# Agent attention and a squared-ReLU feed-forward on one core: other fixed steps for the attention's matmuls among the feed-forward's

## Chip, cores and metric

One core of a Trainium2 chip runs the whole program. The metric is the device time of one execution in microseconds (us), as the median of several runs; lower is better.

## What is computed

Attention goes through 49 agent rows per batch (B = 4, N = 12480, C = 128), and its output feeds a two-layer network with 2048 hidden units:

```python
def _attn_ref(q, k, v, agents):
    scale = 1.0 / np.sqrt(q.shape[-1])
    def sm(a, b):
        s = scale * (a @ b.transpose(0, 2, 1))
        e = np.exp(s - s.max(-1, keepdims=True))
        return e / (e.sum(-1, keepdims=True) + 1e-09)
    agent_v = sm(agents, k) @ v
    return (sm(q, agents) @ agent_v)

h = x @ w_in                      # x: attention's output, 49920 x 128
r = np.maximum(h, 0.0)
out = (r * r) @ w_out
```

## The kernel before

The kernel never forms the attention's output. For each batch it multiplies `agent_v` by `w_in` once (`w_make`), which gives weights with 49 rows, and the feed-forward's first matmul then runs on the softmax of the queries' scores.

**The main loop** (lines 586 to 597) has NG = 832 steps. Step i runs `mm1(i)`, 6 matmuls of 480 columns in row halves, then `relu` on ScalarE (ACT), and at odd i `square` on ACT, `high` and `low` on VectorE (DVE), which split the squares in a rounded part and a rest. `mm2` follows LAG = 5 steps later with 12 matmuls. 16 steps (NF) are a *group*: 960 queries, two output tiles of 8 steps (NJ) each. I count *places* 0 to 15 in a group from the step in which `mm2` begins its first output tile: step = 5 + 16 g + place. `mm2` begins an output tile at places 0 and 8, and `store` takes it at 7 and 15: a copy on ACT, an addition on DVE (L398), a DMA from SP.

**The two PSUM pairs.** `pairs` (line 145) are two tiles of two banks. While `mm2` sums an output tile in one, the other is the scratch of every attention matmul (`bank`, `use`, line 388); at the next output tile they change roles. So an attention matmul on the scratch pair waits until the reader of the one before has finished; the first in an output tile waits for `store`'s addition; and `mm2` of the next output tile waits for the reader of the last.

**The attention's steps**, each a matmul on PE and its reader:

- `q_scores` (32 matmuls in the profile, L167), read on DVE by `q_shift`: a maximum (L299) and a subtraction (L304). Then `q_exp` (ACT), `q_inverse` (DVE, L315 to L320), `q_norm` (GpSimd, L323), `q_hi` (ACT), `q_lo` (GpSimd, L330).
- `q_transpose`, row turning (16 matmuls, L338), read on ACT by `q_copy` (two copies, L342); then two DMAs `q_spread` (L347) make the half-swapped copy `p_b`.
- `k_scores` (L167), read on ACT by `k_copy` (L174), then `k_pmax` on DVE.
- `v_acc`, the sum of values of one tile of 960 rows (16 matmuls, L226), read on DVE by `v_sum` (L240 the first of a batch, L242 the others). Ahead of it go `v_hi` (ACT), `v_lo` (DVE, L218), `k_sub`, `k_lo` (GpSimd), `k_exp`, `k_hi` (ACT).
- `w_make` (L277), read by four copies on ACT (L283) and four subtractions on DVE (L285); `k_max` and `a_final` are short.

**The order** is fixed in advance: functions are put at step numbers by `at`, sorted, and recorded in that order, and every engine runs its own instructions in it. `chain` (line 417) places a list of operations one after another: each goes at least `hop` steps behind the one before, ACT and DVE get at most one attention operation a step (`taken`), and a PE operation is only put in a step of the set `slots`. A PE operation's reader must come in the next step. An attention operation stands at step + 0.5, behind that step's `mm2`. `plan_tokens` (line 447) plans a group's queries, with `q_load` 6 steps ahead of the scores; `plan_batch` (line 457) plans the next batch's keys, values and weights, and the batch after it starts where the values end. Two of the lines:

```python
    slots = {i for i in range(LAG, NG) if (i - LAG) % NJ in (1, 3, 5)}
        plan_tokens(s, (s - 2) * NF + NF // 2 + LAG)
```

So before, the places 1, 3, 5, 9, 11, 13 are open to all kinds. In the order that comes of it `q_scores` stands at 9 and `q_transpose` at 1 in every group; of 39 `v_acc`, 12 stand at 3, 4 at 5, 18 at 11 and 5 at 13; `k_scores` stand at 3, 5 and 11, `w_make` at 11 and 3.

Of the kernel before, what the change touches and what calls it, by code (L numbers as in the profile page):

```python
# [25 lines left out]
def agent_attention_relu2_kernel(ctx: ExitStack, tc: tile.TileContext, qT, kT, v, agT, w_in, w_out, outT):  # L26
# [12 lines left out]
    NF = F // P  # L39
    NJ = NF // 2  # L40
# [310 lines left out]
    NG = NSG * NF  # L351
# [50 lines left out]
    LAG = 5  # L402
# [3 lines left out]
    def at(t, f, *args):  # L406
        steps.append((t, len(steps), f, args))
# [3 lines left out]
    hop = {"PE": {"PE": 1, "ACT": 1, "DVE": 1}, "ACT": {"PE": 2, "ACT": 1, "DVE": 0, "POOL": 0, "SP": 0},  # L411
           "DVE": {"PE": 2, "ACT": 1, "DVE": 1, "POOL": 1, "SP": 0}, "POOL": {"PE": 3, "ACT": 2, "DVE": 2, "POOL": 1}}
    ends = {i for i in range(NG + LAG) if i >= LAG and (i - LAG) % NJ == NJ - 1}
    slots = {i for i in range(LAG, NG) if (i - LAG) % NJ in (1, 3, 5)}
    taken = {(e, i) for i in ends for e in ("ACT", "DVE")}

    def chain(t, todo):

        first = prev = None
        while todo:
            n = 1
            while todo[0][0] == "PE" and n < len(todo) and todo[n][1] in reads_bank and todo[n][0] != "PE":
                n += 1
            t += hop[prev][todo[0][0]] if prev else 0
            while True:
                g, p, ts = t, None, []
                for e, *_ in todo[:n]:
                    g += hop[p][e] if p else 0  # L430
                    while (e, g) in taken or (e == "PE" and g not in slots):
                        g += 1
                    ts.append(g)
                    p = e
                if todo[0][0] != "PE" or ts[-1] <= ts[0] + 1:
                    break
                t += 1
            for (e, f, *args), g in zip(todo, ts):
                taken.add((e, g))
                at(g + .5, f, *args)  # L440
            first = ts[0] if first is None else first
            prev, t, todo = p, ts[-1], todo[n:]
        return first, t
# [3 lines left out]
    def plan_tokens(s, base):  # L447
        todo = [("PE", q_scores, s), ("DVE", q_shift, s), ("ACT", q_exp, s), ("DVE", q_inverse, s),
                ("POOL", q_norm, s), ("ACT", q_hi, s), ("POOL", q_lo, s),
                ("PE", q_transpose, s), ("ACT", q_copy, s)]  # L450
        first, end = chain(base, todo if s > 1 else todo[2:])
        if s > 1:
            at(first - 6, q_load, s)
        at(end + .9, q_spread, s)
        assert end + 3 < s * NF, (s, end)

    def plan_batch(b, base):

        end = b * NS * NF
        for n in range(NS):  # L460
            if b == 1 and n < AHEAD:
                continue
            first, t = chain(base + int(n * 4.6), [("PE", k_scores, b, n), ("ACT", k_copy, n), ("DVE", k_pmax, n)])
            at(max(base, first - 8), k_load, b, n)
            if n == NS - 2:
                chain(t + 1, [("DVE", k_max, 0)])
        _, t0 = chain(t + 1, [("DVE", k_max, 1), ("PE", k_max, 2), ("DVE", k_max, 3), ("PE", k_max, 4), ("DVE", k_max, 5)])
        free = {}
        d = (end - 37 - t0) / NS
        for n in range(NS):  # L470
            t, r = t0 + 1 + int(n * d), free.get(n - 2, 0) + 1
            first, _ = chain(max(t - 2, r), [("ACT", v_hi, n, 0), ("DVE", v_lo, n, 0)])
            _, t2 = chain(max(t - 1, r), [("ACT", v_hi, n, 1), ("DVE", v_lo, n, 1)])
            at(first - 6, v_load, b, n)
            _, t1 = chain(max(t, r - 3), [("POOL", k_sub, n), ("ACT", k_exp, n), ("ACT", k_hi, n), ("POOL", k_lo, n)])
            _, t = chain(max(t1 + 3, t2 + 2), [("PE", v_acc, n), ("DVE", v_sum, n)])
            free[n] = t - 1
        _, e = chain(t + 1, [("DVE", a_final, 0, b), ("PE", a_final, 1, b), ("DVE", a_final, 2, b)])
        for f in range(0, F // 512, 2):
            _, e = chain(e + 2, [("PE", w_make, b, (f, f + 1), 0), ("ACT", w_make, b, (f, f + 1), 1), ("DVE", w_make, b, (f, f + 1), 2)])  # L480
        assert e + 2 < end, (e, end)
        return t + 1
# [95 lines left out]
        at(t - 2 + .1 * x, wo_split, 3, x)  # L578
    plan_tokens(1, 0)
    for s in range(2, NSG):  # L580
        plan_tokens(s, (s - 2) * NF + NF // 2 + LAG)
    t = 0
    for b in range(1, B):
        t = plan_batch(b, t)
# [41 lines left out]
```

## Time and profile before

| | |
|---|---|
| runs | 1997.25, 1997.75, 2004.7 us (median 1997.75) |
| profiled execution | 1994.79 us, of it 1993.0 us from first to last instruction |
| mean granted TensorE clock | 0.996 of full |
| TensorE busy | 1963.5 us |
| VectorE busy | 1762.7 us |
| ScalarE busy | 1725.0 us |
| GpSimd busy | 308.2 us |
| DMA | 129.56 MB, 65 GB/s on average |

The main loop begins at about 74 us and fills the rest. Its stages: in groups 0 to 38 the next batches' work is done beside the queries', three times keys, then values, then weights; from group 39 (1545 us) on only queries' work is left. A busy TensorE is one that has a matmul in its pipeline; a wait for a semaphore shows as idle time only beyond the matmuls still in flight.

### The profile page before, as it was taken

The numbers are of one execution on the slowest core, as the hardware profiler recorded it, in microseconds if no ns is written. First come the engines' busy times: TensorE is split into PE (matmuls) and PEld (weight loads), VectorE is DVE, ScalarE is ACT, GpSimd is POOL, SyncE is SP. The second block draws the span as 40 slices with busy tenths as digits, with TensorE's granted clock in tenths as the row PEclk, the third lists the DMA queues.
The fourth block names the chain that finished last, engine by engine and source line by source line (L and its number), as shares of the span: only waits on it lengthen the run. The fifth ranks groups of instructions, "written<-read, shape, count | busy, mean of one in ns | idle before, by whom it ended". The sixth has DMA issues, their size and how long they took to land.

```text
span 1993.0 us, 45859 instructions
## 1 busy us (share of the span) xinstructions
PE 1963.5 (99%) x20130; PEld 1852.2 (93%) x20130; DVE 1762.7 (88%) x1513; ACT 1725.0 (87%) x1818; POOL 308.2 (15%) x199
## 2 busy tenths in 40 slices
PE   9999999999999999999999999999999999999999
PEld 8699989999889999999979999899998999999998
DVE  7788899999888889999987888999998989888887
ACT  2588899998888889999988889899998999999997
POOL 0100122331000003332100000232210101010110
PEclk9999999999999999999999999999999999999999
DMA  8422122121122122122122212222211111111110
GB/s 289 122 84 81 43 76 74 54 76 54 44 85 83 48 61 74 48 81 64 43 66 69 73 54 70 60 64 68 62 47 37 34 51 29 51 33 51 34 42 21
DMA packets 52849, 129.56 MB, mean 65 GB/s; under 512 B 5761, under 2 KB 21249, under 8 KB 52649
## 3 DMA queue, kind: packets, MB, share of 16 engines
q1 hardware_dynamic: 52648, 126.62, 22.1%
q8 instruction: 158, 2.59, 0.5%
q14 instruction: 43, 0.34, 0.1%
HBM read 81.47 MB, written 25.56 MB: 54 GB/s over the span
## 4 chain that ended last, share of the span: by engine, by line
PE 74%; DVE 10%; ACT 10%; issue 5%; DMA 0%; DVEq 0%; SPq 0%; ACTq 0%
PE pair L392 40%; PE h L364 22%; PE pair L167 7%; ACT rg L373 4%; ACT rg L370 4%; DVE gl L381 3%; DVE gh L377 3%; PE pair L338 2%; DVE vs L218 1%; PE pair L226 1%; PE h L167 1%; PE pair L277 1%; PE pair L494 1%; DMA vt<-v 0%; DVE e L304 0%
## 5 line engine op out<-in xcount | busy, mean ns | idle before, releaser
L370 ACT ACTIVATE rg<-h 128x960 f32<-128x960 f32 x832 | 806.3, 976 | 193.3 <-PE h L364 191.9
L381 DVE TENSOR_TENSOR gl<-rg,gh 128x1920 fp32r<-128x1920 f32 x416 | 916.1, 2202 | 19.0 <-DVE gh L377 0.5
L373 ACT ACTIVATE rg<-rg 128x1920 f32<-128x1920 f32 x416 | 758.0, 1822 | 6.1
L392 PE MATMUL pair<-gh,wo_hi 64*128 64x480 f32 x3328 | 681.6, 377 | 5.7 <-DVE acc L240 5.1
L392 PE MATMUL pair<-gh,wo_lo 64*128 64x480 f32 x3328 | 682.4, 378 | 0.0
L377 DVE CAST gh<-rg 128x1920 fp32r<-128x1920 f32 x416 | 518.2, 1246 | 149.8 <-ACT rg L373 144.2
L364 PE MATMUL h<-p_b,w_hi 49*128 49x480 f32 x1664 | 643.4, 387 | 0.0
L364 PE MATMUL h<-p_a,w_hi 49*128 49x480 f32 x1664 | 640.6, 387 | 0.2
L392 PE MATMUL pair<-gl,wo_hi 64*128 64x480 f32 x3328 | 522.5, 376 | 0.4 <-DVE gl L381 0.3
L392 PEld LDWEIGHTS pair<-gh,wo_hi 64*128 64x128 f32 x3328 | 362.5, 184 | 23.1 <-DVE acc L240 6.4
L392 PEld LDWEIGHTS pair<-gh,wo_lo 64*128 64x128 f32 x3328 | 365.4, 186 | 16.5
L392 PEld LDWEIGHTS pair<-gl,wo_hi 64*128 64x128 f32 x3328 | 355.2, 185 | 15.9 <-DVE gl L381 1.2
L364 PEld LDWEIGHTS h<-p_a,w_hi 49*128 49x128 f32 x1664 | 306.9, 185 | 16.1 <-issue 6.9
L364 PEld LDWEIGHTS h<-p_b,w_hi 49*128 49x128 f32 x1664 | 307.2, 185 | 7.4
L364 PE MATMUL h<-p_a,w_lo 49*128 49x480 f32 x832 | 313.0, 376 | 0.0
L364 PE MATMUL h<-p_b,w_lo 49*128 49x480 f32 x832 | 312.6, 376 | 0.0
L323 POOL TENSOR_TENSOR e<-e,sm 120x392 f32<-120x392 f32 x52 | 54.5, 1048 | 1225.6 <-DVE sm L320 1132.3
L364 PEld LDWEIGHTS h<-p_a,w_lo 49*128 49x128 f32 x832 | 156.1, 188 | 3.2
L364 PEld LDWEIGHTS h<-p_b,w_lo 49*128 49x128 f32 x832 | 156.0, 188 | 2.3
L330 POOL TENSOR_TENSOR pp<-e,pp 120x392 fp32r<-120x392 f32 x52 | 104.0, 1999 | 95.7 <-ACT pp L327 95.6
L206 POOL TENSOR_TENSOR pe<-sk,pe 120x392 fp32r<-120x392 f32 x39 | 78.6, 2016 | 257.9 <-ACT pe L203 210.3
L167 PEld LDWEIGHTS pair<-ag_sb,qt 64*120 64x120 f32 x1600 | 94.2, 181 | 1.2
(93 smaller groups left out, 1342.7 us busy)
## 6 DMA issues: line engine op xcount, KB each, us to landing
vt<-v SPq DMA_DIRECT2D x104, 243.8 KB
kt<-kT SPq DMA_DIRECT2D x52, 480.0 KB
qt<-qT SPq DMA_DIRECT2D x52, 480.0 KB
outT<-ob SPq DMA_DIRECT2D x104, 240.0 KB
p_b<-p_a SPq DMA_DIRECT2D x104, 183.8 KB
raw<-w_in SPq DMA_DIRECT2D x4, 512.0 KB
raw<-w_out SPq DMA_DIRECT2D x4, 512.0 KB
ag_sb<-agT SPq DMA_DIRECT2D x1, 196.0 KB
```

The costliest lines, as they stand in the source:

```text
L167: nc.tensor.matmul(ps[:CH, u, c * A:(c + 1) * A], x[rg[u], h, c, :], ag_sb[rg[u], b, h, :], start=h == 0, stop=h == 1)
L206: eng.tensor_tensor(out=pes[n][:, :, A:], in0=piece(n), in1=pes[n][:, :, :A].bitcast(F32), op=ALU.subtract)
L218: eng.tensor_tensor(out=vs[:, :, C + 2:], in0=vts[n][:, halves[h], :C], in1=vs[:, :, :C].bitcast(F32), op=ALU.subtract)
L323: eng.tensor_tensor(out=es[s], in0=es[s], in1=sms.pop(s).to_broadcast([CH, G, A]), op=ALU.mult)
L330: eng.tensor_tensor(out=pps[s][:, :, L:], in0=es.pop(s), in1=pps[s][:, :, :A].bitcast(F32), op=ALU.subtract)
L338: nc.tensor.matmul(pss["t", s][u][:, c, :], pp[rc[u], c, :], ident_r[rc[u], rc[u]], start=True, stop=True)
L364: nc.tensor.matmul(h[:, u, :TT], w[ra[u], j, :], PT[s][u ^ lo][ra[u], cs, :], start=x == 0, stop=x == 2)
L370: nc.scalar.activation(rgs[p][:, x], hs.pop(i)[:, :, :TT], AF.Relu)
L373: nc.scalar.activation(rgs[p], rgs[p], AF.Square)
L377: nc.vector.tensor_copy(ghs[p], rgs[p])
L381: nc.vector.tensor_tensor(out=gls[p], in0=rgs.pop(p), in1=ghs[p].bitcast(F32), op=ALU.subtract)
L392: nc.tensor.matmul(outs[t][u][:, :TT], w[rg[u], 2 * j + e, :], g[rg[u], e, :], start=j == 0 and x == 0, stop=j == NJ - 1 and x == 5)
```

## The change

Three edits in the plan; no operation is added or removed.

```diff
-    slots = {i for i in range(LAG, NG) if (i - LAG) % NJ in (1, 3, 5)}
+    slots = {q_scores: (5,), q_transpose: (3,), v_acc: (1, 9, 13)}
...
-                    while (e, g) in taken or (e == "PE" and g not in slots):
+                    while (e, g) in taken or (e == "PE" and (g - LAG) % NF not in slots.get(todo[0][1], (1, 9, 11, 13))):
...
-        plan_tokens(s, (s - 2) * NF + NF // 2 + LAG)
+        plan_tokens(s, (s - 2) * NF + LAG)
```

Each kind now has its own places of the 16: `q_scores` 5, `q_transpose` 3, `v_acc` 1, 9 or 13, all others 1, 9, 11 or 13. The planning of a group's queries begins 8 steps earlier; scores come 4 steps earlier than before and row turning 2 steps later. In the new order 9 `v_acc` stand at 1, 23 at 9 and 7 at 13; `k_scores` at 1, 9, 11 and 13, up to four in a group; `w_make` at 1 and 9. The first batch's values lie in groups 4 to 10 (before 5 to 10), the second's in 15 to 23 (before 17 to 23), the third's in 28 to 36 (before 30 to 36).

On DVE, before, around the sums of values in group 9: `vs` is `v_lo`, `mx` and `e` are `q_shift` at place 10, `acc` is `v_sum`, `gh` and `gl` are `high` and `low`, `ob` is the store at 7.

```order
L398 TENSOR_TENSOR ob<-ob,pair_104 128x480
L381 TENSOR_TENSOR gl<-rg,gh 128x1920
L218 TENSOR_TENSOR vs_83<-vt,vs_83 120x4x128
L377 CAST gh<-rg 128x1920
L381 TENSOR_TENSOR gl<-rg,gh 128x1920
L218 TENSOR_TENSOR vs_83<-vt,vs_83 120x4x128
L299 TENSOR_REDUCE mx<-pair_104 120x8
L304 TENSOR_TENSOR e<-pair_104,mx 120x392
```

And now, from the store at place 15 of group 4 to `v_sum` at place 2 of group 5:

```order
L398 TENSOR_TENSOR ob<-ob,pair_105 128x480
L381 TENSOR_TENSOR gl<-rg,gh 128x1920
L218 TENSOR_TENSOR vs_82<-vt,vs_82 120x4x128
L377 CAST gh<-rg 128x1920
L381 TENSOR_TENSOR gl<-rg,gh 128x1920
L218 TENSOR_TENSOR vs_82<-vt,vs_82 120x4x128
L242 TENSOR_TENSOR acc<-pair_105,acc 98x516
```

The queue ahead of the pair's reader is the same; the reader is one sum where it was `q_shift`'s two instructions, and `q_transpose` waits for it where `v_acc` did.

On DVE, before, ahead of the first sum of the second batch, at place 14 of group 17, from `q_shift` at 10 on:

```order
L304 TENSOR_TENSOR e<-pair_104,mx 120x392
L377 CAST gh<-rg 128x1920
L381 TENSOR_TENSOR gl<-rg,gh 128x1920
L315 TENSOR_REDUCE sm<-e 120x8
L319 TENSOR_SCALAR sm<-sm 120x8
L320 RECIPROCAL sm<-sm 120x8
L218 TENSOR_TENSOR vs_83<-vt,vs_83 120x4x128
L377 CAST gh<-rg 128x1920
L381 TENSOR_TENSOR gl<-rg,gh 128x1920
L218 TENSOR_TENSOR vs_83<-vt,vs_83 120x4x128
L240 COPY acc<-pair_104 98x516
```

And now, ahead of the sum at place 14 of group 20, from place 8 on:

```order
L319 TENSOR_SCALAR sm<-sm 120x8
L320 RECIPROCAL sm<-sm 120x8
L377 CAST gh<-rg 128x1920
L381 TENSOR_TENSOR gl<-rg,gh 128x1920
L377 CAST gh<-rg 128x1920
L381 TENSOR_TENSOR gl<-rg,gh 128x1920
L218 TENSOR_TENSOR vs_83<-vt,vs_83 120x4x128
L377 CAST gh<-rg 128x1920
L381 TENSOR_TENSOR gl<-rg,gh 128x1920
L218 TENSOR_TENSOR vs_83<-vt,vs_83 120x4x128
L242 TENSOR_TENSOR acc<-pair_104,acc 98x516
```

The two `v_lo` are still there, while `q_shift` and the row sums (`sm`) have moved one casting pair or more ahead of them.

On ACT, before, around the second `w_make` of the second batch (group 12): `w_hi` are the four copies at place 4, `p_a` is `q_copy` at 2, `sk` is `k_copy` at 6.

```order
L342 CAST p_a<-pair_105 113x8x64
L342 CAST p_a<-pair_105 113x8x56
L373 ACTIVATE rg<-rg 128x1920
L370 ACTIVATE rg<-h 128x960 x2
L283 CAST w_hi<-pair_105 49x256 x4
L373 ACTIVATE rg<-rg 128x1920
L370 ACTIVATE rg<-h 128x960 x2
L174 COPY sk<-pair_105 120x392
```

And now, around the first one (group 11), with `w_hi` at place 2 and `q_copy` at 4:

```order
L283 CAST w_hi<-pair_105 49x256 x4
L373 ACTIVATE rg<-rg 128x1920
L370 ACTIVATE rg<-h 128x960 x2
L342 CAST p_a<-pair_105 113x8x64
L342 CAST p_a<-pair_105 113x8x56
L373 ACTIVATE rg<-rg 128x1920
L370 ACTIVATE rg<-h 128x960 x2
```

Row turning now comes two steps behind `w_make`, on the same pair, where the keys' scores did.

## The prediction

> **What bounds the kernel now.** I read the page first, then the list of waits, then a window of one group in each stage, and last the timeline around each wait that ends on TensorE. On the page:
>
> ```profile
> span 1993.0 us, 45859 instructions
> PE 1963.5 (99%) x20130; PEld 1852.2 (93%) x20130; DVE 1762.7 (88%) x1513; ACT 1725.0 (87%) x1818; POOL 308.2 (15%) x199
> ```
>
> TensorE (PE) has work in hand for all but 29.5 us. The change removes no matmul, so only such gaps, and what hides in them, can be won. The waits of PE inside the loop name their cause (total us, times, longest):
>
> ```profile
> PE pair L226 <- DVE e L304: 8.8, 13, 1.3
> PE pair L392 <- DVE acc L240: 5.1, 3, 2.5
> PE pair L167 <- DVE w_lo L285: 3.1, 4, 1.0
> PE pair L338 <- DVE ob L398: 0.6, 1, 0.6
> PE pair L392 <- DVE acc L242: 0.5, 1, 0.5
> ```
>
> All five are one thing (out tile and line of who waits, of whom): a matmul that wants the PSUM pair whose last content VectorE (DVE) has not finished reading. The stages differ; a window's row gives the stretch, its length, busy us of PE, PEld, DVE, ScalarE (ACT) and GpSimd, then the granted clock, the DMA share and GB/s:
>
> ```profile
> 1545.40:1579.30 33.90, 33.90 (x339) 31.36 (x339) 30.96 (x25) 31.15 (x31) 3.87 (x2) 1.00 0.14 42
> 796.80:833.80 37.00, 36.05 (x370) 33.60 (x369) 36.37 (x31) 34.80 (x40) 11.35 (x6) 1.00 0.23 65
> 833.80:870.60 36.80, 35.93 (x370) 35.30 (x368) 34.28 (x30) 34.38 (x38) 11.18 (x6) 1.00 0.23 65
> ```
>
> The first row is a late group with queries alone: PE busy 33.90 of 33.90 us, nothing to win. The other two are groups with two value tiles each: PE lacks 0.9 us, and DVE is busy 36.37 of 37.00 us in one of them. So the prize lies in the stages of values and of weights, and DVE's lag there sets it.
>
> **Part 1: `v_acc` no longer follows the queries' scores.** Before, 18 of the 39 value sums stand at place 11, two steps behind `q_scores` at 9. The worst of them, DVE and then PE, from the timeline (start us, duration us):
>
> ```profile
> 448.65 0.64 DVE L398 TENSOR_TENSOR ob<-ob,pair 128x480 f32<-128x480 f32 x1
> ...
> 453.07 2.16 DVE L381 TENSOR_TENSOR gl<-rg,gh 128x1920 fp32r<-128x1920 f32 x1
> 455.14 0.68 DVE L218 TENSOR_TENSOR vs<-vt,vs 120x512 fp32r<-120x512 f32 x1
> 455.75 0.56 DVE L299 TENSOR_REDUCE mx<-pair 120x8 f32<-120x392 f32 x1
> 456.41 0.57 DVE L304 TENSOR_TENSOR e<-pair,mx 120x392 f32<-120x392 f32 x1
> ...
> 455.24 0.61 PE L392 MATMUL pair<-gl,wo_hi 64*128 64x480 f32 x4
> 457.12 1.21 PE L226 MATMUL pair<-vs,pe 64*98 64x258 f32 x16 [1.27 <-DVE e L304]
> ```
>
> L304 ends at 456.98, L226 starts at 457.12. The profile counts 1.27 us idle; by starts it is 1.46, since the four matmuls from 455.24, two pairs 0.22 apart, were through at about 455.66. So each wait is worth some 0.2 us more than its row. The 13 waits are 8.8 + 13 x 0.2 = 11.4 us, and all go: no `v_acc` stands behind `q_scores` now.
>
> What is late next is the sum behind a sum. In 9 places `v_acc` at 1 is followed by `q_transpose` at 3, which waits for `v_sum`. Ahead of that read stand the same rows as above: 5 of the 9 have both `v_lo` (L218) in places 0 and 1, as that case had them at 8 and 9. The reader is shorter: L299 to L304 took 1.23 us (455.75 to 456.98), the sum takes 0.64:
>
> ```profile
> 949.94 0.64 DVE L242 TENSOR_TENSOR acc<-pair,acc 98x516 f32<-98x516 f32 x1
> ...
> 950.89 0.30 PE L226 MATMUL pair<-vs,pe 64*98 64x258 f32 x2
> ```
>
> But PE arrives sooner too, since what it does between the two is the sum's own matmuls and no longer the scores':
>
> ```profile
> L167 PE MATMUL pair<-ag_sb,qt 64*120 64x49 f32 x1600 | 90.5, 261 | 0.0
> ...
> L226 PE MATMUL pair<-vs,pe 56*98 56x258 f32 x312 | 44.9, 283 | 0.0
> ```
>
> 90.5 us for 50 scores are 1.81 each, 44.9 for 39 sums 1.15. The two shifts (0.59 and 0.66) cancel, so I take the mean of the old waits, 8.8/13 + 0.2 = 0.88, for the five, and 0.2 for the four with fewer `v_lo`: 5.2 us. Bounds: 0, since here a sum at 11 held up nothing at 13 (read over at 950.58, next matmul at 950.89), and 9 x 1.46 = 13.
>
> **Part 2: `v_acc` at 13, output matmuls at 0.** Before, 5 value sums stand at 13; the worst two cost this:
>
> ```profile
> 768.23 2.93 POOL L330 TENSOR_TENSOR pp<-e,pp 120x392 fp32r<-120x392 f32 x1
> ...
> 767.55 2.73 DVE L381 TENSOR_TENSOR gl<-rg,gh 128x1920 fp32r<-128x1920 f32 x1
> 770.20 1.50 DVE L218 TENSOR_TENSOR vs<-vt,vs 120x512 fp32r<-120x512 f32 x1
> 771.63 0.68 DVE L240 COPY acc<-pair 98x516 f32<-98x516 f32 x1
> ...
> 772.37 0.48 PE L392 MATMUL pair<-gh,wo_hi 64*128 64x480 f32 x2 [2.44 <-DVE acc L240]
> ```
>
> Both had `q_shift` (1.23) and the row sums on DVE just ahead, at 10 and 11:
>
> ```profile
> L315 DVE TENSOR_REDUCE sm<-e 120x8 f32<-120x392 f32 x52 | 28.8, 554 | 1.5 <-ACT e L311 1.5
> ...
> L320 DVE RECIPROCAL sm<-sm 120x8 f32<-120x8 f32 x52 | 10.6, 203 | 1.8
> ```
>
> The L240 and L242 rows give 5.1 + 0.5 + 4 x 0.2 = 6.4 us, and L338's 0.8 goes with them, since places 1 and 9 now come behind a lighter DVE. Now 7 stand at 13. Two of them still have two `v_lo` ahead, without those 1.23 + 0.55 + 0.20 us: 2.44 - 1.98 + 0.2 = 0.66 each, 1.3 us. The other five have one `v_lo` or none: 0. Bounds 0 and 7 x 2.6 = 18.
>
> L218 took 1.50 instead of 0.68 us beside GpSimd's L330. The Trainium skill ("SBUF — State Buffer", Who interferes with whom) calls the port that the two share an exclusive lock, under which the second to start waits out the first. By that rule each of the two `v_lo` could lose the whole 2.93 us, and my two places would cost 4 us more; the row shows 0.82, which I keep.
>
> **Part 3: weights.** `w_make` leaves DVE four subtractions on its pair:
>
> ```profile
> 554.63 1.73 DVE L285 TENSOR_TENSOR w_lo<-pair,w_hi 49x256 fp32r<-49x256 f32 x4 [1.37 <-ACT w_hi L283]
> ...
> 556.42 1.88 PE L167 MATMUL pair<-ag_sb,kt 64*120 64x49 f32 x32 [0.95 <-DVE w_lo L285]
> ```
>
> Before, two of the six `w_make` of the loop have another matmul on the pair two steps later (at 3, then `k_scores` at 5). Now five have: three at 1 with `q_transpose` at 3, two at 9 with `k_scores` at 11. Three more at 0.95 + 0.2: 3.5 us more. Bounds: 0, and twice that, 7.
>
> A long wait has a second price here, the granted clock (the column behind the engines):
>
> ```profile
> 1047.00:1052.00 5.00, 5.00 (x34) 4.30 (x34) 3.24 (x3) 3.71 (x4) 0.00 (x0) 0.66 0.00 0
> 1262.00:1267.00 5.00, 4.30 (x26) 3.68 (x28) 5.00 (x6) 2.37 (x3) 0.00 (x0) 0.66 0.14 51
> ```
>
> One follows the second `w_make` wait, one the second 2.4 us wait: 5 x 0.34 = 1.7 us each, one in two of each kind. Five such `w_make` waits make 2.5 losses for the 2 of before: 0.9 us more. Bounds: 3.4 less (no loss left) and 5 more (a loss at each of the five). The Trainium skill ("TensorE: Matmul & The Clock Gate", What's actually happening) lets the clock fall after an idle window of about 3.4 us. By that no wait here would lower it, and the sum would be 3.4 us better than before instead; the trace has the lower clock behind a wait of about 1 us, so I go by the trace.
>
> **Part 4: queries.** `q_scores` moves from 9 to 5, `q_transpose` from 1 to 3, in 50 groups. First cover: scores at 5 wait for ScalarE's copies of the transposes. With the same two steps between, before:
>
> ```profile
> 359.62 1.03 ACT L342 CAST p_a<-pair 113x512 fp32r<-113x512 f32 x2
> ...
> 361.82 0.43 PE L226 MATMUL pair<-vs,pe 64*98 64x258 f32 x4
> ```
>
> The copies end 1.17 us ahead: 0 us, and if ScalarE falls behind by more, that excess. Second: the output matmuls at 8 need `q_shift` read. The nearest rows, a group of the keys' stage:
>
> ```profile
> 154.27 0.57 DVE L304 TENSOR_TENSOR e<-pair,mx 120x392 f32<-120x392 f32 x1
> ...
> 155.80 0.42 PE L167 MATMUL pair<-ag_sb,kt 64*120 64x49 f32 x6
> ```
>
> 0.96 us spare at two steps; from 5 to 8 an `mm1` more, a third of a step (33.90/16 = 2.1 us), makes 1.6. In the value stage the old lag of up to 1.46 eats most of that: in five groups a `v_lo` stands right ahead, 0.2 each, 1.0 us. Third: the store at 7 now has `q_shift` ahead on DVE. Behind the store of 448.65 PE took the pair here:
>
> ```profile
> 450.06 0.53 PE L167 MATMUL pair<-ag_sb,qt 64*120 64x49 f32 x8
> ```
>
> L398 was over at 449.29, 0.77 us ahead, and `q_shift` is done before the square that the cast ahead of L398 waits for: 0. The last `q_transpose` comes two steps nearer its use, 8 steps instead of 10, against a DMA `q_spread`. SP issues a keys' load right behind a store:
>
> ```profile
> 485.84 0.43 SPq L161 DMA_DIRECT2D kt<-kT  x1
> ...
> 487.80:489.80 2.00, 2.00 (x35) 2.00 (x35) 1.97 (x2) 0.50 (x1) 0.00 (x0) 1.00 0.50 189
> 489.80:491.80 2.00, 2.00 (x22) 2.00 (x20) 1.90 (x3) 1.78 (x2) 0.00 (x0) 1.00 0.00 0
> ```
>
> Its traffic is over within 4 us of the issue, so neither `q_spread` (six steps of about 2 us left) nor the load that is now planned in the very step of its scores (place 11; SP reaches it behind the store of 7) is late. If that cover fails, one load costs some 4 us, twice.
>
> **Sum.** Gone: 11.4 + 6.4 + 0.8 = 18.6. New: 5.2 + 1.3 + 3.5 + 0.9 + 1.0 = 11.9. Net 6.7, and since values now spread over more groups in the second and third batch (13 over 9 groups, not over 7), I put it at 8. The profiled execution took 1994.79 us, 1.79 more than its span; the runs' median is 1997.75, 3 above it. 1997.75 - 8 = 1989.7 us, 0.4% faster. A measurement of this kernel can tell about 0.5%, 10 us, from no change.
>
> **Rivals.** *The new waits hardly come* (DVE, relieved at 10 and 11, keeps up): 18.6 less some 3 for the weights, 15.6 us, about 1982. For it: the sum of the L242 row held up nothing. Against it: five places have the very queue of the worst case. *The waits only move*: nine waits of 1.2 in part 1 and 7 us of the other new ones are 17.8 against 18.6: 1997 us, no change. For it: DVE at 36.37 of 37.00 us. Against it: the window after that one leaves DVE 2.5 us. *Slower*: `q_shift` at 6 becomes late for the output matmuls at 8 in all 50 groups, because ScalarE's two copies (1.03 us by their row), now at 4, push square, cast and `low` ahead of it. It decides from the point where DVE reaches `q_shift` more than 1.6 us later than in the keys' row; at 0.5 us a group, 25 - 8 = 17 us more, 2015 us. Against it: PE gets the transposes' and scores' time too, so ScalarE's net delay is under 0.5 us.
>
> **How the numbers follow.** Forecast 0.50 (1985 to 1994 us, a third of it past 10 us gained), the new waits hardly come 0.24, waits only move 0.12, slower 0.14. Faster by over 0.5%: 0.24 + 0.17 = 0.41. Slower by over 0.5%: 0.14 + 0.02 = 0.16. Between: 0.43. The range takes in the first rival, with the bounds of parts 1 to 3 at their good ends, down to 1978, and above the second and the near part of the third, up to 2003.
>
> **What would show it.** Right: L226 <- L304 gone from the waits; L338 <- L242 there with about 5 us; L338 <- L285 three times at 1 us; late groups still 33.9 us. Wrong: L392 <- L304 in many groups (the slower rival), L364 waiting for ScalarE's L370, or L167 waiting for its load.

## The result and the profile after

| | before | after |
|---|---|---|
| median of six runs each, us | 2002.8 (1997.25 to 2020.23) | 2033.8 (2030.4 to 2040.0) |
| profiled execution, us | 1994.79 | 2035.38 |

The ratio is 1.0153, with a 95% interval of 1.012 to 1.0185. The kernel is slower, and the forecast of 1989.7 us with its range up to 2003 was wrong.

The head of the page after the change:

```profile
span 2033.3 us, 45870 instructions
PE 1983.2 (98%) x20130; PEld 1837.2 (90%) x20130; DVE 1792.2 (88%) x1513; ACT 1725.5 (85%) x1818; POOL 353.6 (17%) x199
```

No engine got an instruction more (the x counts are those of before), yet DVE is busy 29.5 us longer and GpSimd 45.4 us longer. So the same operations take longer. The waits of PE name what ends late:

```profile
PE pair L392 <- DVE gl L381: 11.6, 14, 1.1
PE pair L392 <- DVE acc L242: 8.3, 7, 2.0
PE pair L338 <- DVE acc L242: 7.9, 7, 1.2
PE pair L167 <- DVE w_lo L285: 4.7, 4, 2.1
PE pair L338 <- DVE w_lo L285: 3.2, 3, 1.1
```

L226 <- L304, 8.8 us before, is gone, as forecast. The first row is new in kind: it is no wait for a PSUM pair. The output matmuls (L392) stand waiting for `low` itself (L381), the rest of the squares that they multiply. Before, PE lost 0.3 us to it in the whole loop. Now nine of the 14 waits, of 1.07 to 1.14 us each, stand at place 0, in just the nine groups that have a sum of values at 1. Here is one case, DVE around the sum of place 10 in group 5 and on to the end of that group (start us, duration us):

```profile
317.02 2.68 DVE L381 TENSOR_TENSOR gl<-rg,gh 128x1920 fp32r<-128x1920 f32 x1
319.62 1.45 DVE L218 TENSOR_TENSOR vs<-vt,vs 120x512 fp32r<-120x512 f32 x1
321.00 0.68 DVE L242 TENSOR_TENSOR acc<-pair,acc 98x516 f32<-98x516 f32 x1
321.60 1.14 DVE L377 CAST gh<-rg 128x1920 fp32r<-128x1920 f32 x1
322.78 2.88 DVE L381 TENSOR_TENSOR gl<-rg,gh 128x1920 fp32r<-128x1920 f32 x1
325.58 1.44 DVE L218 TENSOR_TENSOR vs<-vt,vs 120x512 fp32r<-120x512 f32 x1
326.95 1.92 DVE L377 CAST gh<-rg 128x1920 fp32r<-128x1920 f32 x1
328.98 2.16 DVE L381 TENSOR_TENSOR gl<-rg,gh 128x1920 fp32r<-128x1920 f32 x1
```

GpSimd in the same microseconds:

```profile
316.10 1.58 POOL L323 TENSOR_TENSOR e<-e,sm 120x392 f32<-120x392 f32 x1 [5.79 <-DVE sm L320]
317.65 2.88 POOL L196 TENSOR_TENSOR sk<-sk,mM 120x392 f32<-120x392 f32 x1
321.25 2.40 POOL L330 TENSOR_TENSOR pp<-e,pp 120x392 fp32r<-120x392 f32 x1 [0.72 <-ACT pp L327]
325.50 0.97 POOL L206 TENSOR_TENSOR pe<-sk,pe 120x392 fp32r<-120x392 f32 x1 [1.85 <-ACT pe L203]
326.44 1.41 POOL L196 TENSOR_TENSOR sk<-sk,mM 120x392 f32<-120x392 f32 x1
```

`low` takes 2.16 us where GpSimd is idle (the last DVE row) and 2.68 or 2.88 beside it, `v_lo` (L218) 1.45 instead of 0.68, a cast 1.92 instead of 1.14. I call what an operation takes over its quiet length its *stretch*. And PE at the start of the next output tile, group 6 place 0:

```profile
329.67 0.38 PE L392 MATMUL pair<-gh,wo_lo 64*128 64x480 f32 x2
331.19 0.71 PE L392 MATMUL pair<-gl,wo_hi 64*128 64x480 f32 x4 [1.14 <-DVE gl L381]
```

The last `low` ends at 331.14 and the matmul that reads it starts at 331.19. Over the whole run the groups say the same; first of before (mean ns of one behind the busy time), then of after:

```profile
L381 DVE TENSOR_TENSOR gl<-rg,gh 128x1920 fp32r<-128x1920 f32 x416 | 916.1, 2202 | 19.0 <-DVE gh L377 0.5
...
L218 DVE TENSOR_TENSOR vs<-vt,vs 120x512 fp32r<-120x512 f32 x78 | 59.2, 768 | 0.0
```

```profile
L381 DVE TENSOR_TENSOR gl<-rg,gh 128x1920 fp32r<-128x1920 f32 x416 | 956.1, 2298 | 22.8 <-DVE gh L377 0.5
...
L218 DVE TENSOR_TENSOR vs<-vt,vs 120x512 fp32r<-120x512 f32 x78 | 69.7, 899 | 0.0
```

L381's 40 us more (956.1 against 916.1) and L218's 10.5 are more than all that DVE gained in busy time; the casts (L377) gave 19.4 back, 498.8 against 518.2.

**Where the time went, place by place.** The waits say who was late, not what it came to. So I took the start of every block of matmuls in the loop (an `mm1`, an `mm2`, an attention operation) and the distance to the next one, less the ordinary distance (0.648 us for `mm1`, 1.296 for `mm2`, 1.600 for scores, 0.955 for a sum of values, 0.721 for row turning, 1.902 for `w_make`). Summed over all steps at one place of the group this is the place's *lateness*, in us:

| | loop | place 0 | 3 and 4 | 8 | 11 | 14 |
|---|---|---|---|---|---|---|
| before | 59.1 | 9.0 | 4.8 | 1.0 | 13.7 | 2.3 |
| after | 92.0 | 27.5 | 27.6 | 0.5 | 3.6 | 6.4 |

The loop lost 33.0 us, and the medians differ by 31.0. Place 11 gave back 10.1. Place 0 lost 18.5, places 3 and 4 lost 22.8, place 14 lost 4.1, all others together gained 2.5. (In the profiled execution the loop also began at 80.2 us, not 74.3. The program ahead of it is unchanged, and over all runs below that start lies anywhere from 73.6 to 80.2; I count it as chance.)

### The profile page after: what moved, and what is told of

Same layout as the page of the kernel before. It is cut to its first block, busy times and chain, and to the rows that moved or that the text cites. A ratio compares the mean times of both kernels' runs of the same rounds, so it can differ in the third digit from the quotient of the medians.

```text
span 2033.3 us, 45870 instructions
## 1 busy us (share of the span) xinstructions
PE 1983.2 (98%) x20130; PEld 1837.2 (90%) x20130; DVE 1792.2 (88%) x1513; ACT 1725.5 (85%) x1818; POOL 353.6 (17%) x199
## 4 chain that ended last, share of the span: by engine, by line
PE 68%; DVE 18%; issue 8%; ACT 4%; DMA 1%; SPq 0%; DVEq 0%; ACTq 0%
PE pair L392 36%; PE h L364 20%; PE pair L167 7%; DVE gl L381 6%; DVE gh L377 5%; DVE vs L218 3%; ACT rg L370 2%; PE pair L338 2%; DVE acc L242 1%; ACT rg L373 1%; DVE ob L398 1%; PE h L167 1%; DMA vt<-v 1%; PE pair L494 1%; PE pair L277 1%
## 5 line engine op out<-in xcount | busy, mean ns | idle before, releaser
L381 DVE TENSOR_TENSOR gl<-rg,gh 128x1920 fp32r<-128x1920 f32 x416 | 956.1, 2298 | 22.8 <-DVE gh L377 0.5
L392 PE MATMUL pair<-gh,wo_hi 64*128 64x480 f32 x3328 | 699.5, 379 | 8.3 <-DVE acc L242 8.3
L392 PE MATMUL pair<-gh,wo_lo 64*128 64x480 f32 x3328 | 699.7, 379 | 0.0
L364 PE MATMUL h<-p_b,w_hi 49*128 49x480 f32 x1664 | 630.7, 389 | 0.0
L377 DVE CAST gh<-rg 128x1920 fp32r<-128x1920 f32 x416 | 498.8, 1199 | 141.4 <-ACT rg L373 131.9
L392 PE MATMUL pair<-gl,wo_hi 64*128 64x480 f32 x3328 | 541.0, 379 | 12.2 <-DVE gl L381 11.6
L392 PEld LDWEIGHTS pair<-gh,wo_hi 64*128 64x128 f32 x3328 | 391.1, 185 | 33.6 <-DVE acc L242 11.2
L392 PEld LDWEIGHTS pair<-gh,wo_lo 64*128 64x128 f32 x3328 | 394.0, 187 | 21.7
L392 PEld LDWEIGHTS pair<-gl,wo_hi 64*128 64x128 f32 x3328 | 365.2, 186 | 41.3 <-DVE gl L381 21.8
L323 POOL TENSOR_TENSOR e<-e,sm 120x392 f32<-120x392 f32 x52 | 80.8, 1554 | 1116.8 <-DVE sm L320 960.3
L330 POOL TENSOR_TENSOR pp<-e,pp 120x392 fp32r<-120x392 f32 x52 | 101.8, 1958 | 154.8 <-ACT pp L327 154.7
L196 POOL TENSOR_TENSOR sk<-sk,mM 120x392 f32<-120x392 f32 x39 | 91.7, 2352 | 37.0 <-DVE mM L193 37.0
```

What stands on the lines that cost most here:

```text
L196: eng.tensor_tensor(out=piece(n), in0=piece(n), in1=m.rearrange("p (o a) -> p o a", o=1).to_broadcast([CH, G, A]), op=ALU.subtract)
L323: eng.tensor_tensor(out=es[s], in0=es[s], in1=sms.pop(s).to_broadcast([CH, G, A]), op=ALU.mult)
L330: eng.tensor_tensor(out=pps[s][:, :, L:], in0=es.pop(s), in1=pps[s][:, :, :A].bitcast(F32), op=ALU.subtract)
L364: nc.tensor.matmul(h[:, u, :TT], w[ra[u], j, :], PT[s][u ^ lo][ra[u], cs, :], start=x == 0, stop=x == 2)
L377: nc.vector.tensor_copy(ghs[p], rgs[p])
L381: nc.vector.tensor_tensor(out=gls[p], in0=rgs.pop(p), in1=ghs[p].bitcast(F32), op=ALU.subtract)
```

## The experiments

Three theories stood against each other. *Spacing*: where the matmuls stand is wrong, a sum of values at 1 with row turning at 3 above all. *Contention*: what moved with them is wrong; GpSimd's `q_norm` and `q_lo` now run at 9 to 11 among the keys' operations, stretch DVE there, and `low` comes late at place 0. *Balance*: TensorE's attention work has left the second half of a group, so DVE has less cover there. Each experiment's ratio is to the kernel before, run on the same chip. Lateness of all of them, in us, beside the two rows above:

| | ratio, 95% interval | loop | place 0 | 3 and 4 | 8 | 11 |
|---|---|---|---|---|---|---|
| after, sums not at 1 | 1.0006 [0.9985, 1.0027] | 63.7 | 22.9 | 11.4 | 0.5 | 2.6 |
| after, no low parts | 0.9966 [0.9947, 0.9986] | 58.7 | 6.5 | 20.1 | 1.2 | 3.6 |
| before, no low parts | 0.9949 [0.9920, 0.9977] | 50.4 | 7.7 | 4.4 | 1.2 | 4.1 |
| after, both cures | 0.9903 [0.9865, 0.9941] | 46.1 | 7.2 | 10.2 | 1.2 | 2.6 |
| after, GpSimd's part later | 1.0079 [1.0051, 1.0106] | 75.6 | 7.4 | 38.3 | 0.5 | 3.6 |
| before, planned 8 steps earlier | 1.0095 [1.0078, 1.0111] | 77.5 | 4.3 | 17.1 | 22.2 | 0.8 |
| before, sums at 3, 5, 13 | 0.9983 [0.9960, 1.0005] | 59.1 | 14.4 | 4.3 | 2.9 | 0.9 |
| before, sums at 3, 5 | 1.0095 [1.0079, 1.0111] | 80.8 | 21.8 | 3.7 | 3.6 | 0.9 |
| before, scores at 11 | 1.0016 [0.9989, 1.0044] | 62.9 | 2.5 | 16.0 | 6.9 | 12.1 |
| before, 11 and 13 become 12 | 0.9916 [0.9885, 0.9946] | 48.7 | 11.5 | 4.3 | 1.3 | 0.1 |
| before, turning 2, sums 4, 12 | 0.9964 [0.9936, 0.9991] | 55.6 | 10.9 | 8.0 | 1.4 | 0.0 |
| before, GpSimd dose | 1.0043 [1.0015, 1.0070] | 76.4 | 14.8 | 5.5 | 2.2 | 16.2 |

**1. Sums of values not at 1.**

```diff
-    slots = {q_scores: (5,), q_transpose: (3,), v_acc: (1, 9, 13)}
+    slots = {q_scores: (5,), q_transpose: (3,), v_acc: (9, 13)}
```

> The changed kernel with the sums of values at 9 and 13 only (24 and 15 of them), so none stands at 1 ahead of row turning at 3. Three theories of why the change costs some 30 us. S (spacing): the cost is the sum at 1 with row turning two steps behind it, nine waits of 1.4 us and the half clock after some of them. Then the waits L338 <- L242 go and the time falls by 15 to 20 us, to about 1.006 of the kernel before. C (contention): VectorE is late in places 9 to 15 because GpSimd's four operations of queries and values run there side by side with it; then what VectorE still owes shows at place 0, the waits of the output matmuls for the sum at 14 grow, and the time stays within 8 us of the changed kernel (1.011 to 1.019). B (balance): places 8 to 15 hold too little of TensorE's attention work against VectorE's; a second sum there gives TensorE 1 us more per group but takes VectorE 0.65 us, so the time falls a little, 3 to 8 us (about 1.012).

2003.1 us: all of the loss is gone, more than any of the three theories had. Its waits:

```profile
PE pair L392 <- DVE acc L242: 8.4, 10, 1.7
PE pair L392 <- DVE gl L381: 6.2, 7, 1.1
```

L338 <- L242 is out of the list, and places 3 and 4 fall from 27.6 to 11.4 us. But place 0 is still 22.9 us late, and `low` as slow as after the change:

```profile
L381 DVE TENSOR_TENSOR gl<-rg,gh 128x1920 fp32r<-128x1920 f32 x416 | 955.9, 2298 | 23.3 <-PE pair L167 0.5
```

So the sums at 1 explain places 3 and 4. Of place 0's loss of 18.5 us only 4.6 go with them: the waits for `low` halve, 7 rows for 14, while the sums at 13 double.

**2 and 3. The low parts left out**, of the kernel after and of the kernel before. `k_lo` and `q_lo` on GpSimd do nothing; zeros stand in their place, so that part of the computation is left out:

```diff
-        eng.tensor_tensor(out=pes[n][:, :, A:], in0=piece(n), in1=pes[n][:, :, :A].bitcast(F32), op=ALU.subtract)
+        pass
...
-        eng.tensor_tensor(out=pps[s][:, :, L:], in0=es.pop(s), in1=pps[s][:, :, :A].bitcast(F32), op=ALU.subtract)
+        es.pop(s)
```

> The changed kernel without GpSimd's two subtractions that make the low parts of the exponentials and of the normalised rows (those low parts stay zero); every other instruction and every step is the same. C (contention): 91 GpSimd operations of 2 us are gone, so VectorE's low (L381) falls from a mean of 2298 ns to near 2200, the waits at place 0 and for L242 mostly go, and the time falls to within 10 us of the kernel before without the same two subtractions (run beside it). B (balance): VectorE's own work is the same, the waits stay, and the time is 25 us or more above that kernel. S (spacing): the nine waits L338 <- L242 stay at over 1 us each.

> The kernel before without the same two subtractions of GpSimd (those low parts stay zero), the partner of the run with them left out of the changed kernel. C: somewhat faster than the kernel before, by 5 to 12 us, as the waits L226 <- L304 lose what GpSimd's side by side work adds to VectorE; B and S: within 5 us of the kernel before.

1996.2 and 1992.9 us: without these operations the two orders are 3.3 us apart, where it was 31. The waits of the kernel after without them (its lines are numbered 5 higher: L343 is row turning, L247 the sum, L397 the output matmuls, L386 `low`):

```profile
PE pair L343 <- DVE acc L247: 8.0, 7, 1.2
...
PE pair L397 <- DVE acc L247: 2.4, 3, 1.1
...
PE pair L397 <- DVE gl L386: 0.2, 1, 0.2
```

The wait for `low` fell from 11.6 to 0.2 us, `low` itself from 2298 to 2227 ns, and place 0 from 27.5 to 6.5 us, while row turning waits for the sums as long as before (8.0 for 7.9). The matmuls stand where the change put them in all of this. So place 0's loss is contention's, and balance alone does not make it.

**4. Both cures at once**, to see whether they act on the same waits.

> The kernel after the change with both cures at once: sums of values at 9 or 13 alone, and the low parts of the attention weights (k_lo and q_lo on GpSimd) left out, zeros in their place. Each alone took 28 to 33 us of lateness out of the loop's 92. If they act on different waits, both together leave some 31 us, and the time is 1963 to 1972 us. If each removed the same waits (a sum at 1 costs only where VectorE is already stretched), little is left for the second: 45 to 57 us of lateness and 1984 to 1994 us.

1985.0 us, lateness 46.1 us: inside the range of the second outcome, at its lower end, so the two cures overlap. They are not the same cure, as the places show: with the low parts out, the sums still take places 3 and 4 from 20.1 to 10.2; with the sums away, the low parts still take place 0 from 22.9 to 7.2. But the gains fall 15.7 us short of adding up (28.3 and 33.3 alone, 45.9 together), 5.3 of it at place 0 and 6.3 at places 3 and 4. About 8.5 us can be traced: of the six stretches at half clock in the loop after the change (1.7 us each, see below) none is left in experiment 1, one in experiment 2 and none here, so five of them go only once. The rest is open.

**5. The kernel after, with GpSimd's part of the queries six steps later**, out of places 9 to 11:

```diff
-        first, end = chain(base, todo if s > 1 else todo[2:])
+        if s > 1:
+            first, end = chain(base, todo[:4])
+            _, end = chain(end + 6, todo[4:])
+        else:
+            first, end = chain(base, todo[2:])
```

> The changed kernel with the queries' GpSimd part later: q_norm at 14 instead of 9, q_hi and q_lo at 0 instead of 11; matmuls keep their places, sums of values at 1, 9 and 13 as before in the same numbers. C: VectorE's casting and subtraction at 9 to 13 meet at most two GpSimd operations instead of four, the nine waits at place 0 shrink by half or more, and the time falls by 8 to 15 us (1.007 to 1.011). B and S: the same within 5 us (1.012 to 1.018).

2017.6 us. Place 0 falls to 7.4 us without any matmul having moved, which is contention's claim once more (the copy `q_hi` on ScalarE, which stands between the two GpSimd operations, moved with them). But the work now runs at 14 to 0, ahead of the sums at 1, and their readers are later instead:

```profile
PE pair L338 <- DVE acc L242: 15.5, 9, 2.3
```

Of the 20.1 us that place 0 won, places 3 and 4 gave 10.7 back.

**6. One part of the change on the kernel before: planning 8 steps earlier.**

```diff
-        plan_tokens(s, (s - 2) * NF + NF // 2 + LAG)
+        plan_tokens(s, (s - 2) * NF + LAG)
```

> The kernel before with one part of the change alone: a group's queries planned eight steps earlier, the steps for each kind left as they were (scores at 1, row turning at 9; sums of values at 3 in 11 cases, at 5 in 17, at 11 in 4, at 13 in 7). Both theories: GpSimd's work for the queries only moves from 12 to 14 over to 4 to 6, so L381 stays at 2.19 to 2.22 us and the time at 1998 to 2007 us beside 2002.5. Spacing theory: the wait of the sums behind the scores (L226 on L304) comes in 11 groups in place of 18, 5 to 7 us. If the time is 2015 or more, the early planning itself is the cost, and neither theory holds.

2017.5 us, which neither theory had. The mean of `low` is near the old one (2211 ns), as both said. The waits:

```profile
PE pair L226 <- DVE e L304: 10.3, 11, 1.2
PE pair L392 <- DVE acc L242: 9.3, 7, 1.7
PE pair L392 <- DVE acc L240: 6.9, 3, 2.5
```

The scores stand at 1 now, and the planner deals 17 sums to place 5 (before, 5 stood at the like place 13). In ten groups the first output matmuls at 8 are late, by 0.9 to 4.0 us; place 8 lost 21.2 us. My expectation had taken a sum at 5 for free. What the mean of 416 `low` hides stands in these groups: GpSimd's `q_norm` and `q_lo` now run at 4 to 6, among the keys' operations and just ahead of the sum. DVE and then GpSimd in group 18:

```profile
796.66 1.80 DVE L377 CAST gh<-rg 128x1920 fp32r<-128x1920 f32 x1
798.57 2.74 DVE L381 TENSOR_TENSOR gl<-rg,gh 128x1920 fp32r<-128x1920 f32 x1
801.23 1.51 DVE L218 TENSOR_TENSOR vs<-vt,vs 120x512 fp32r<-120x512 f32 x1
...
797.41 1.88 POOL L196 TENSOR_TENSOR sk<-sk,mM 120x392 f32<-120x392 f32 x1
799.34 2.85 POOL L330 TENSOR_TENSOR pp<-e,pp 120x392 fp32r<-120x392 f32 x1
```

In nine of the ten groups DVE's operations between the scores and the sum are stretched by 1.5 to 2.7 us, 18.3 us together. So contention comes back here at another place, and both theories missed that. I read the cost as that of the deal, not of the early planning: experiment 1 plans as early with the sums dealt otherwise and loses nothing, but it moves scores and row turning as well.

**7 and 8. The other part alone: sums away from the scores**, with scores at 9 and turning at 1 as before. The first with 20 sums at 13, the second with all at 3 or 5. For room, both also put the weights' matmuls one step closer together, and the second the keys' scores 3 steps apart instead of 4.6:

```diff
+    slots = {q_scores: (9,), q_transpose: (1,), v_acc: (3, 5, 13)}
...
+                    while (e, g) in taken or (e == "PE" and (g - LAG) % NF not in slots.get(todo[0][1], (3, 5, 11, 13))):
```

> The kernel before with the other part alone: queries' scores stay at 9 and row turning at 1, so GpSimd's work for the queries stays at 12 to 14, and only the sums of values leave place 11 (3 in 16 cases, 5 in 3, 13 in 20; the weights' matmuls stand one step closer together, for room). The wait of L226 on L304, 8.8 us and some more that it hides, must go. Spacing theory: the 20 sums at 13 cost what they did after the change, 1.2 to 2.0 us each at place 0, 24 to 40 us in all against a gain of 11: 2015 to 2031 us. Contention theory: a sum at 13 cost that much only where VectorE was already stretched; L381 stays at 2.19 to 2.22 us, a sum at 13 costs 0 to 0.5 us, and the time is 1991 to 2002 us.

> As the run before this, with all sums of values at 3 or 5 (21 and 18), where neither the scores stand just ahead nor a sum on VectorE falls before place 0; the keys' scores lie 3 steps apart in place of 4.6, for room. VectorE's v_lo falls mostly at 5, 8, 9 and 12, and k_lo of GpSimd at 13 in 12 cases. Spacing theory: both waits go, 1985 to 1992 us. Contention theory: much the same gain, less what the denser GpSimd work at 12 to 14 costs: L381 at 2.20 to 2.25 us, 1988 to 2002 us.

The first took 1996.4 us: the wait behind the scores is gone (13.7 to 0.9 us at place 11), and the 15 sums more at 13 cost 5.4 us at place 0, some 0.4 each; after the change the seven waits for a sum at 13 came to 8.3 us, 1.2 each. I take it that a sum at 13 is dear where DVE is already behind, as contention had it. (Place 5 lost another 5.0 us, 3.4 of it one wait of the keys' scores.) The second took 2019.5 us against both expectations:

```profile
PE pair L392 <- DVE gl L381: 14.4, 19, 1.5
```

With the sums at 3 and 5 the planner put 18 `v_lo` at 8 and 18 at 12, and DVE had too much to do between 8 and 15: place 0 lost 12.8 us, by `low`. The mean of `low`, 2219 ns, again hides the stretch: in the 18 halves of a group that end late, DVE's operations took 2.4 us over their quiet lengths, nearly as much as in the 20 such halves after the change, 2.7. So DVE's load in that half and contention act together here. Place 5 lost another 12.4 us, half of it in two waits of the keys' scores, 3.1 us for their load and 3.0; so this run is not one of the sums' places alone, and whether the closer keys made those waits is not shown.

**9, 10 and 11. Other spacings on the kernel before.** Scores at 11, turning at 3, sums at 5 and 9; then places 11 and 13 closed and 12 opened instead, which moves the 23 sums that stood there to 12 (20 of them) and 3, and the keys' scores and weights from 11 to 12; then turning at 2 with sums at 4 and 12. The second is the smallest:

```diff
+    slots = {q_scores: (9,), q_transpose: (1,), v_acc: (3, 5, 12)}
...
+                    while (e, g) in taken or (e == "PE" and (g - LAG) % NF not in slots.get(todo[0][1], (3, 5, 12))):
```

> The kernel before with the scores of the queries at 11, row turning at 3, sums of values at 5 or 9 (22 and 17) and the rest at 1, 5, 9 or 13. Neither row turning nor the scores stand behind a sum of values. GpSimd's query work falls at 14 to 0, apart from the keys' in most groups. Spacing theory: the waits of L226 on L304, L338 on L242 and at place 0 all go, 1985 to 1993 us. Contention theory: GpSimd's work next to VectorE's low at 14 to 0 stretches L381 to 2.23 to 2.27 us, and the time is 1995 to 2010 us.

> The kernel before with what stood at place 11 moved to 12 and nothing else: scores of the queries at 9, row turning at 1, sums of values at 3, 5 or 12 (15, 4 and 20). GpSimd's work for the queries stays at 12 to 14, and the split of TensorE's work between a group's halves stays. If the wait behind the scores is a gain that can be had for nothing, L226 on L304 goes, the lateness at place 11 (13.7 us of the loop) falls to 1 to 3, and the time is 1989 to 1995 us beside 2000. If the sum, now on VectorE at 13, makes the first output tile of the next group late instead, as after the change, place 0 takes what place 11 gave: 1998 to 2004 us.

> As the run before this, with row turning at 2, sums of values at 4 or 12 (18 and 21) and the keys' scores at 0, 4 or 12, so that three or four steps lie between two attention matmuls in nearly all groups. Spacing theory: waits for VectorE behind them (L226 on L304, L338 on L242) all go, 1986 to 1993 us. Contention theory: k_lo of GpSimd now gathers at 2 and 9 in front of the queries' work at 12 to 14, L381 at 2.21 to 2.26 us, 1990 to 2002 us.

2001.6, 1986.9 and 1993.8 us. In the first the waits only moved, to the scores behind a sum at 9:

```profile
PE pair L167 <- DVE acc L242: 5.5, 9, 1.1
```

The second beats both kernels of this study: 0.9916 [0.9885, 0.9946]. Its waits of the output matmuls, with no row of L226 on L304 left:

```profile
PE pair L392 <- DVE acc L242: 4.1, 3, 1.4
PE pair L392 <- DVE acc L240: 2.8, 3, 1.0
```

Three steps between scores and sum are enough, place 11 falls from 13.7 to 0.1 us, and place 0 takes back only 2.5. So the gain that the change was priced at was there to be had, with the queries' GpSimd work at 12 to 14 and the halves' balance left as they were. The third came out where contention had it (1990 to 2002 us), with `low` at 2259 ns; place 0 stayed at 10.9 us, and place 2, where row turning now stands, lost 10.2. `low` is slower in the second and third than in experiments 6 and 8, and they are faster: its mean alone does not tell the time, it matters in which groups it is slow.

**12. A dose of GpSimd work on the kernel before**, read by nobody:

```diff
+    def dummy(s):
+        for _ in range(8):
+            nc.gpsimd.tensor_tensor(out=dum, in0=dum, in1=mkeep[s].to_broadcast([CH, G, 12]), op=ALU.subtract)
+
+    for s in range(2, NSG):
+        at((s - 2) * NF + LAG + 10.55, dummy, s)
```

> The kernel before with nothing moved and one thing added: in each of 50 groups eight small operations on GpSimd (120x96, both inputs in SBUF, no reader) just behind q_shift at place 10, where the change puts GpSimd's work; some 3 to 4 us of it in a group. TensorE's, VectorE's and ScalarE's instructions stay as they are. Contention theory: L381 grows from 2.20 to 2.23 to 2.30 us, lows are late for place 0 (9.0 us of lateness there before, 15 to 30 now), and the time is 2005 to 2025 us beside 2000. If GpSimd's place does not matter and only the matmuls' places do: L381 at 2.19 to 2.21 us and 1998 to 2003 us.

2014.0 us, in the range of contention, but not by its mechanism alone. The eight took 704 ns each in the mean, 5.6 us a group, more than I had reckoned; where nothing of DVE held them up they took 350 ns, the longest 2187. The waits (lines 3 or 4 higher: L368 is `mm1`, L374 `relu`, L229 the sum, L308 `q_shift`):

```profile
PE h L368 <- ACT rg L374: 11.7, 15, 1.7
PE pair L229 <- DVE e L308: 10.8, 15, 1.8
```

`low` grew only to 2221 ns, less than contention's 2230 to 2300, and place 0 by 5.8 us. The largest row came through ScalarE, where `q_hi` (L331) waited for a `q_norm` (L327) held up behind the dose, with `relu` queued behind it. From ScalarE's waits:

```profile
ACT pp L331 <- POOL e L327: 18.6, 18, 3.3
```

This wait is of the dose's making and has no like after the change. The dose was also cut too fine to act as the kernel's own operations do: DVE's casts, `low` and `v_lo` that met only the dose took at most 0.20 us over their quiet lengths, those that met an operation of the kernel up to 0.84. So the run shows that GpSimd work that nobody reads slows this loop; it does not size the contention.

**DVE's account by half group.** One sum holds these cases together. For the second half of each group (what DVE does between the `low` for place 8 and the one for place 0) I added DVE's busy time, and beside it TensorE's ordinary time for the same eight steps with the attention matmuls planned in them. Means over 50 groups, us; an "overfull" half has DVE busy over 1 us longer than TensorE, a late one is over 0.3 us late at place 0:

| | DVE busy | of it stretch | TensorE | overfull | late | late and overfull |
|---|---|---|---|---|---|---|
| before | 17.6 | 0.5 | 18.0 | 5 | 3 | 2 |
| after | 18.9 | 1.7 | 17.1 | 40 | 20 | 20 |
| after, sums not at 1 | 18.6 | 1.5 | 17.3 | 38 | 19 | 18 |
| after, no low parts | 18.1 | 0.9 | 17.1 | 21 | 3 | 3 |
| before, sums at 3, 5 | 18.9 | 1.1 | 17.4 | 26 | 18 | 18 |
| before, 11 and 13 become 12 | 17.5 | 0.8 | 18.0 | 6 | 8 | 5 |

(Stretch here is counted over the 20th percentile of all runs. A small shift of the bound of 1 us moves the overfull counts, after the change between 35 and 40.) The change took 0.9 us of matmuls out of that half, the scores of the queries among them, and put 1.2 us of stretch into it. In the 20 late halves after the change DVE is 3.7 us over TensorE, 2.7 of it stretch. Balance is thus a part of it, though not enough by itself: without the low parts TensorE's 17.1 stays, and 3 halves are late. The account does not cover experiment 12, where 11 halves are late and none of them is overfull; there the wait came through ScalarE. This is an account made after the fact; that stretch makes the difference is shown by experiments 2 and 5, the part that balance has in it only by this table.

## Why the prediction was wrong

**What was gone** was right. L226 <- L304 is gone, place 11 gave 10.1 us (forecast 11.4), and experiment 10 took that gain nearly alone.

**Part 1, row turning behind a sum at 1,** had the right wait and half its size. Forecast: five of 0.88 and four of 0.2, 5.2 us, bounds 0 to 13. Measured, by starts: seven of the nine late by 0.9 to 1.4 us, the other two by 0.2, some 9.5 us. The step that failed is the price of one: I took the mean of the old waits for the queue that the worst of them had. DVE's rows ahead of the row turning of group 6, which was 1.39 late, are of ordinary length, so there it was the queue, not the stretch, and experiment 2 keeps the wait at 8.0 us:

```profile
334.75 0.68 DVE L218 TENSOR_TENSOR vs<-vt,vs 120x512 fp32r<-120x512 f32 x1
335.36 1.15 DVE L377 CAST gh<-rg 128x1920 fp32r<-128x1920 f32 x1
336.55 2.16 DVE L381 TENSOR_TENSOR gl<-rg,gh 128x1920 fp32r<-128x1920 f32 x1
338.62 0.69 DVE L218 TENSOR_TENSOR vs<-vt,vs 120x512 fp32r<-120x512 f32 x1
339.23 0.69 DVE L242 TENSOR_TENSOR acc<-pair,acc 98x516 f32<-98x516 f32 x1
```

**Part 2, sums at 13,** failed as a step. "The other five have one v_lo or none: 0" and the two at 0.66, 1.3 us in all; measured 8.3 us in seven rows. The argument was that DVE is relieved, as `q_shift` and the row sums have moved ahead. They had, but `q_norm` and `q_lo` moved with them from 12 and 14 to 9 and 11, into the steps of `k_sub`, `k_lo` and the crowd of `v_lo`. That step was not in the sum: part 4 followed the queries' matmuls, copies, loads and spread, and never GpSimd's two operations. Without the low parts, or with GpSimd's part later, the sums at 13 cost 2.4 and 2.7 us in three rows each, so most of the 8.3 is that step's. I had a row in hand that told of it (L218 at 1.50 us beside L330), used it only for two places, and misread it. I set its 0.82 against the whole 2.93 us of L330; but L218 began at 770.20 and L330 ended at 771.16, so only 0.96 us of L330 were left to wait for, and 0.82 is nearly all of that.

**What the sum did not hold at all** is the largest row of the list: L392 waiting for `low`, 11.6 us in 14. I looked for late readers of PSUM pairs, since all five waits of before were of that kind. Once DVE falls behind by more than the distance of `low` to its matmul, the output matmul of place 0 waits, pair or no pair, as it did in nine groups.

**Part 3, weights:** 3.2 us in three rows, forecast 3.5 more. Right. The clock was forecast at 0.9 us. Behind the first 20 us of the loop, where both kernels have one (3.4 us before, 6.8 after, which I had not counted), six stretches at half clock lie in the loop, for two before: 4 x 1.7 = 6.8 us, above its bound of 5. I had tied them to the weights' waits; all six follow a wait for a sum, five of them row turning at 3, one the output matmuls at 0. By my estimate those five are some 8.5 us of what places 3 and 4 lost; with part 1's 9.5 and part 3's 3.2 + 3 x 0.2 that is nearly all of the 22.8. One of them, around the row turning of group 6 (stretch, length, busy PE, PEld, DVE, ACT, GpSimd, clock, DMA share, GB/s):

```profile
336.00:341.00 5.00, 3.80 (x44) 3.08 (x42) 4.95 (x5) 3.58 (x4) 0.00 (x0) 1.00 0.06 19
341.00:344.40 3.40, 3.40 (x20) 2.81 (x20) 2.16 (x1) 2.19 (x4) 0.00 (x0) 0.50 0.00 0
```

**Part 4, queries,** was right where it looked: no wait of L392 for L304, place 8 at 0.5 us, no load late, and late groups still 33.9 us. Of the rivals, "slower" came with another mechanism than mine: 1.5% and not 0.9, at place 0 and not at 8.

**Left open:** why the loop's start varies by 6 us from run to run, what part of place 0's loss is balance, and 7 us of the overlap of the two cures.

## What to carry over

When an operation moves in a hand-made order, write down the whole chain that moves with it, with each engine's old and new place, and look at what runs on the neighbour engine there. Count each part of the loop as a balance, busy time of the engine that feeds against busy time of the engine that is fed; an engine at 88% over the run was over 100% in one half of a group. Look at an operation's length in the groups that end late: its mean over the run hid the stretch twice. And try the smallest move that removes a wait first: here closing 11 and 13 for 12 won 0.8%, the full rearrangement lost 1.5%.

## What the hardware showed

Of two operations on DVE and GpSimd that overlap, one waited out the other. With nothing beside them, `low` takes 2.16 us, the cast 1.16, `v_lo` 0.68, and GpSimd's L196 0.95 (at 1270.39 in the trace of before). In group 5 above, `low` began at 317.02 beside an L323 that ended at 317.68, and took 0.52 longer. L196 began at 317.65 and took 1.93 longer; `low` ended at 319.70. `v_lo` began at 319.62 and took 0.77 longer; L196 ended at 320.53. Each lost what was left of the other, less some 0.14 us. That holds over the whole loop after the change: in all 149 casts, `low` and `v_lo` that took over 0.2 us more than their quiet lengths, and in all 155 such GpSimd operations, the loss is the rest of the other engine's operation less 0.12 to 0.15 us (5th to 95th percentile). Which one waits does not follow from the recorded starts alone: L323 had begun before `low`, but the cast at 321.60 kept its length inside an L330 that began at 321.25, and that L330 took 2.40 us. The sum (L242) and `q_shift`, which read PSUM, never stretched; no L242 took over 0.69 us.

The Trainium skill ("SBUF — State Buffer", Who interferes with whom) calls their shared port an exclusive lock. The trace agrees with that.

The clock fell to half for 3.4 us behind a wait of 1.2 us (the row turning at 339.97, in the windows above); in the 3.41 us ahead of the fall PE was busy for 2.21. The Trainium skill ("TensorE: Matmul & The Clock Gate", What's actually happening) asks for an idle window of about 3.4 us. The length of the slow stretch agrees with that figure; the idle time needed does not, here as in the trace of before.
